# Keys and values of two chunks in one load: a retention layer with a SoLU network behind it

## The chip, the cores and the metric

The kernel runs on one core of a Trainium2 chip. The metric is the device time of one launch in microseconds (us), as the median of several runs. Beside the timed runs one execution was profiled; its span goes from the first to the last instruction of the program.

## What is computed

For 8 batches and 8 heads, with 576 positions of head size 64, the attention part is a retention layer: scores with a decay per head, causal, no softmax. Its output becomes 4608 tokens of 512 channels, which pass through a network with a SoLU activation and a layer norm:

```
scores = q @ k.T / sqrt(64)
ret    = scores * gamma[h] ** (i - j)      # for i >= j, otherwise 0
x      = ret @ v                           # tokens x 512, heads side by side
h      = x @ w_in                          # 512 -> 1024
solu   = h * softmax(h)
ln     = (solu - mean) / sqrt(var + 1e-6) * g_ln
out    = ln @ w_out                        # 1024 -> 512
```

All inputs and the output are 32-bit floats. Inside, matmul operands are 16-bit floats.

## The kernel before

The work is cut into 36 chunks of 128 tokens. Batches go in four pairs, and each pair has nine chunks: for each of four blocks of 128 positions one chunk of the first batch and one of the second, then a ninth chunk that holds the last 64 positions of both. Chunks 0 to 8 are the first pair, 9 to 17 the second, and so on. Chunks 9 and 10 are thus the same positions of two neighbouring batches, as are 11 and 12, 13 and 14, 15 and 16; chunk 17 stands alone. The decay is carried from block to block by a state of each batch, so a chunk does not need earlier keys and values.

The order of everything is written out by hand in `ORDER`, a list of steps such as `ck:9:g` (step `ck` of chunk 9 on engine g; a is ScalarE, v VectorE, g GpSimd). There is no loop: the list is run from left to right, and each engine takes its instructions in that order. The steps that matter here:

- `ld` loads queries, keys and values of a chunk into three buffers (`qf`, `kf`, `vf`), three DMAs on SyncE's queue, in this order. SyncE also issues the stores of the output (`st`) and the transposes of 16-bit keys by DMA (`kd`, from chunk 12 on).
- `cq`, `ck`, `cv` scale and convert queries, keys and values to 16 bits, mostly on GpSimd (POOL in the profile); they free the loaded buffer.
- `tq`/`tr` turn queries (and keys) on TensorE; `sc` makes the scores, `mk` masks them on VectorE (DVE), `av` multiplies by the values, `fs` adds the product of the queries with the state, and `dk` on POOL makes that state in 16 bits.
- `ex` copies the result out of PSUM, `m1` is the product with `w_in`, `mx`, `xp` and `so` make the maximum, the exponential and the activation, `tu` and `eu` turn it, `sq`, `ra` and `rp` make the norm, `m2` is the product with `w_out`, and `st` scales on ScalarE (ACT) and stores. `rp` is the step that the profile shows as line 583.

The buffers of a name form a ring whose places are also written out: `SLOTS` lists, for each new buffer, which place it takes, and `BANKS` does the same for the four PSUM banks that are not kept for `h`. A step whose place still has a reader waits for it. Loaded buffers of 2 KB per partition: seven for queries, six for keys, seven for values.

The order around the change, with the first loads that it touches (`ld:12`, `ld:9`, `ld:10`, `ld:11`):

```
... ld:7 tu:2 wo:7:g wo:0:a ld:8 wo:5:a
sq:2 ra:1:g tu:4 mk:6 rp:1 ld:12 mx:3 ld:9 eu:2:v m2:1 sq:0 dk:6 ld:10 dk:4 sq:4 cq:8:g eu:4:v
m2:0 cq:7:v st:1 ck:7:a xp:3 ra:0:v cv:7:v mx:5 so:3 mm:0 ld:11 rp:0 st:0 ...
... cv:8:g eq:8:a ... ck:9:g rp:4 sq:3 kv:7 eu:3:a m2:3 cq:9:g ... dk:7 ... cq:11:v ...
```

A key or value load moves rows of 64 floats (256 bytes); a query load (but for chunk 34) moves rows of 1 KB, since four tokens of a head lie together there.

Of the kernel before, what the change touches and what calls it, by code (L numbers as in the profile page):

```python
# [10 lines left out]
FP = mybir.dt.float32  # L11
F16 = mybir.dt.float16
BF16 = mybir.dt.bfloat16
P = 128
H = 8
D = 64
# [3 lines left out]

PLAIN = 5
BY_DMA = 12
BY_PE = (15, 20)
ORDER = """
c1:0 ld:1 ld:0 cq:1:g cv:1:v ck:1:a cq:0:g tq:1 eq:1:av wu:2:2 wu:5:2 ck:0:a cv:0:g sc:1 ld:2 mk:1
# [16 lines left out]
so:7 av:9 sq:6 ex:9:a tr:10 er:10:a cv:10:g ad:9 d3:9 ra:6:v rp:6 cq:13:g sq:7 ra:7:g ck:13:g  # L42
kd:13 m2:6 st:6 mx:8 cv:13:g tu:7 eu:7:a sc:10 mk:10 m1:9 kv:10 ad:10 dk:10 tr:11 xp:8 so:8 av:10
ex:10:a tr:12 er:12:v cv:12:g er:11:a m2:7 tu:8 dk:9 sc:11 mx:9 m1:10 cv:11:g mk:11 av:11 fs:11
ld:15 sq:8 rp:7 ra:8:v eu:8:a kv:11 d3:10 xp:9 cq:17:g rp:8 ex:11:a st:7 m2:8 so:9 tu:9 ad:11
d3:11 dk:11 mx:10 sc:12 cq:14:g ck:14:a kd:14 sq:9 m1:11 eu:9:v xp:10 ck:15:g ld:16 st:8 kv:12
mk:12 ld:19 ra:9:v cv:17:g tr:14 er:14:a tr:13 ad:12 dk:12 so:10 av:12 fs:12 ex:12:a cv:14:g
er:13:a m2:9 sc:13 mx:11 rp:9 xp:11 mk:13 cq:16:g tu:10 eu:10:a ck:17:v m1:12 so:11 sc:14 st:9
mk:14 av:13 ck:16:g sq:10 fs:13 ex:13:a m2:10 ra:10:g rp:10 mx:12 d3:12 kv:13 ad:13 cq:15:g tu:11
# [40 lines left out]
"""  # L90

BANKS = """
01231023102130121321302130213023110231012320132012302301320310312031201320321021312310210231032032
10230123012031203123123031231023102301201023012021032103213013021301023102130213013202130213012103
130132132132130210321032132123230212103201032301231031
"""

RINGS = dict(
    qf=7, kf=6, vf=7, q16=5, k16=6, v16=5, qkT=4, ret0=4, ret1=4, xT=4, t=4, s16=4, s32=4, h=2,
    e=3, u=5, uT=5, o_sb=4,  # L100
)
SLOTS = """
qf 012345601234560135426015324601532460
kf 012345012345012453014523014520314520
vf 012345601234560134625016342051346250
q16 012340123401324103123041203412304132
v16 012341023410234132012041320421320413
k16 012345120345102341502314053210452310
# [40 lines left out]
def kernel(  # L149
# [10 lines left out]
    nc = tc.nc  # L160
# [11 lines left out]
    load = ctx.enter_context(tc.tile_pool(name="load", bufs=6))  # L172
# [10 lines left out]
    chunks = []  # L183
# [6 lines left out]
    def tokens(src, n):  # L190

        bs, c = chunks[n]
        if c < 4:
            return src[bs[0], :, c * P : (c + 1) * P, :].rearrange("h t d -> t h d")
        return src[bs[0] : bs[1] + 1, :, 4 * P :, :].rearrange("b h t d -> t b h d")

    def fours(src, n):

        bs, c = chunks[n]
        if c < 4:  # L200
            return src[bs[0], :, c * P : (c + 1) * P, :].rearrange(
                "(g h) (t a) d -> t g h (a d)", h=2, a=4
            )
        return src[bs[0] : bs[1] + 1, :, 4 * P :, :].rearrange(
            "b (g h) (t a) d -> t b g h (a d)", h=2, a=4
        )
# [25 lines left out]
    def ring(pool, shape, dtype, name):  # L232

        at = int(next(slots[name]))
        assert at < RINGS[name]
        return pool.tile(shape, dtype, tag=f"{name}_{at}", name=name, bufs=1)
# [5 lines left out]
    T = {}  # L242
# [20 lines left out]
    def quads(n):  # L263

        return n != NCH - 2

    def ld(n):

        for key, src in (("qf", q), ("kf", k), ("vf", v)):
            dst = ring(load, [P, H, D], FP, key)  # L270
            if key == "qf" and quads(n) or key == "kf" and chunks[n][1] == 4:
                nc.sync.dma_start(  # L272
                    out=dst.rearrange("p (h a) d -> p h (a d)", h=2), in_=fours(src, n)
                )
            else:
                nc.sync.dma_start(out=dst, in_=tokens(src, n))  # L276
            T[key, n] = dst

    def scaled(n, key, out, table, engine):
# [35 lines left out]
    def tq(n):  # L315

        tp = bank([P, 2, 4, P], F16, "tp")
        for i, src in enumerate((T.pop(("q16", n)), T["k16", n])):
            s2 = src.rearrange("p h d -> p (h d)")
            for hp in range(4):  # L320
                turn(tp[:, i, hp], s2[:, hp * P : (hp + 1) * P])
        T["tp", n] = tp

    def kd(n):
        if chunks[n][1] == 4 or n < BY_DMA or n in BY_PE:
            return
        T["qkT", n] = ring(att, [P, 2, 4, P], F16, "qkT")
        nc.sync.dma_start_transpose(
            out=T["qkT", n][:, 1], in_=T["k16", n].rearrange("p h d -> p (h d)")
        )  # L330
# [6 lines left out]
    def tr(n):  # L337
        if chunks[n][1] == 4 or n < BY_DMA or n in BY_PE:
            return tq(n)
        tp = bank([P, 4, P], F16, "tr")  # L340
        s2 = T.pop(("q16", n)).rearrange("p h d -> p (h d)")
        for hp in range(4):
            turn(tp[:, hp], s2[:, hp * P : (hp + 1) * P])
        T["tp", n] = tp

    def er(n, e="a"):
        if chunks[n][1] == 4 or n < BY_DMA or n in BY_PE:
            return eq(n, e)
        turned(ENG[e], n, T["qkT", n][:, 0], T.pop(("tp", n)))
# [15 lines left out]
    def eq(n, e="v"):  # L365

        qkT = ring(att, [P, 2, 4, P], F16, "qkT")
        tp = T.pop(("tp", n))
        turned(ENG[e[0]], n, qkT[:, 0], tp[:, 0])
        if chunks[n][1] == 4:  # L370
            turned(ENG[e[-1]], n, qkT[:, 1], tp[:, 1])
        else:
            copy(ENG[e[-1]], qkT[:, 1], tp[:, 1])
        T["qkT", n] = qkT
# [493 lines left out]
```

## Time and profile before

| | us |
|---|---|
| median of 3 runs | 212.56 |
| lowest, highest | 212.26, 213.14 |
| the profiled execution | 211.63 |
| its span | 209.9 |
| TensorE's mean granted clock in it | 0.99 |

The profiled execution is 0.93 us faster than the median of the runs. The page gives each engine's busy time, the span in 40 slices of 5.2 us, the DMA queues, and the chain of work that ended last. PE is TensorE, PEld its weight loads, DVE VectorE, ACT ScalarE, POOL GpSimd, SP SyncE. In a timeline a row has its start and length in us, engine, line, operation, output and inputs, and in brackets the idle time before it and what ended that. Names are cut: `q`, `k` and `v` are the 16-bit tensors, `s` the state, `rs` the result of `rp`.

### The profile page before, as it was taken

What the parts mean: (1) busy time and instruction counts of PE and PEld (TensorE: products, weight loads), DVE (VectorE), ACT (ScalarE), POOL (GpSimd) and SP (SyncE); (2) the same over time, 40 slices, a digit from 0 to 9 for tenths busy, and PEclk for the clock granted to TensorE, in tenths of its full rate; (3) what the DMA queues carried; (4) which work ended last, traced back from release to release, by engine and by line L of the source; (5) the groups of instructions that cost most, each with busy time, mean ns of one, the idle gap of its engine ahead of it and who ended that gap; (6) DMA issues with size and microseconds to landing.
All of it is one profiled execution on the core that took longest, in us unless ns stands there. A gap on an engine that the chain in (4) does not pass through costs nothing.

```text
span 209.9 us, 7674 instructions
## 1 busy us (share of the span) xinstructions
PE 196.1 (93%) x3173; PEld 124.8 (59%) x3173; DVE 178.3 (85%) x312; ACT 167.9 (80%) x289; POOL 166.2 (79%) x244
## 2 busy tenths in 40 slices
PE   0887699999999999999999999999999999999993
PEld 0464457665756666667656656676666666565552
DVE  0476979999998899979898899999989998999650
ACT  2424769999779997988899788888798897798982
POOL 5395979978799998896938999799999984938531
PEclk9999889999999999999999999999999999999999
DMA  5999999999999999999999899999999995999264
GB/s 133 262 342 274 257 201 355 241 244 249 227 267 279 218 212 247 265 192 253 181 276 221 159 224 231 223 229 228 174 263 233 173 196 153 194 188 242 67 219 153
DMA packets 107859, 46.94 MB, mean 224 GB/s; under 512 B 91560, under 2 KB 101808, under 8 KB 107824
## 3 DMA queue, kind: packets, MB, share of 16 engines
q1 hardware_dynamic: 107504, 46.28, 98.3%
q8 instruction: 25, 0.41, 0.9%
q10 hardware_dynamic: 320, 0.16, 0.3%
q14 instruction: 10, 0.08, 0.1%
HBM read 32.54 MB, written 9.44 MB: 200 GB/s over the span
## 4 chain that ended last, share of the span: by engine, by line
PE 83%; SPq 5%; DMA 4%; DVE 3%; POOL 2%; issue 0%; ACT 0%; DVEq 0%
PE o L258 29%; PE h L258 27%; PE lp L253 6%; PE sc L383 5%; DMA qf<-in_q_dram 4%; PE x L458 4%; PE x L258 3%; PE tp L253 3%; PE tr L253 2%; SPq L276 2%; PE kp L407 2%; SPq L272 2%; SPq L781 1%; DVE ret L396 1%; DVE nm L514 1%; POOL q L292 1%
## 5 line engine op out<-in xcount | busy, mean ns | idle before, releaser
L258 PE MATMUL h<-w_in,xT 128*64 128x512 f16 x560 | 67.8, 384 | 0.3 <-DVE w_in L245 0.3
L258 PE MATMUL o<-w_c,uT 128*64 128x512 f16 x480 | 56.8, 380 | 0.0
L396 DVE TENSOR_TENSOR ret<-sc,tris 128x512 f16<-128x512 f32 x72 | 46.2, 682 | 4.2 <-PE sc L383 4.2
L258 PEld LDWEIGHTS <-xT 128*64 128x64 f16 x576 | 32.0, 112 | 24.1 <-issue 2.0
L520 ACT ACTIVATE e<-h,nm 128x1024 f32<-128x1024 f32 x35 | 39.3, 1122 | 7.6 <-DVE nm L514 6.5
L514 DVE TENSOR_REDUCE nm<-h 128x1 f32<-128x1024 f32 x35 | 42.6, 1217 | 1.8 <-PE h L258 1.6
L258 PEld LDWEIGHTS <-uT 128*64 128x64 f16 x560 | 30.0, 110 | 23.6
L529 DVE SCALAR_TENSOR_TENSOR u<-h,e 128x1024 f16<-128x1024 f32 x35 | 42.6, 1218 | 1.3 <-ACT e L520 0.8
L292 POOL TENSOR_TENSOR q<-qf,small 128x512 f16<-128x512 f32 x31 | 32.6, 1056 | 6.8 <-DMA qf<-in_q_dram 6.8
L434 POOL TENSOR_TENSOR s<-t,small 128x512 f16<-128x512 f32 x32 | 33.8, 1061 | 3.8 <-DVE t L422 3.6
L557 ACT ACTIVATE sq<-u,su 128x1024 bf16<-128x1024 f16 x30 | 34.6, 1153 | 1.2 <-DVE u L529 1.1
L281 POOL TENSOR_TENSOR v<-vf,small 128x512 f16<-128x512 f32 x32 | 33.8, 1061 | 1.4 <-DMA vf<-in_v_dram 1.3
L617 ACT ACTIVATE o_sb<-o,rs 128x512 f32<-128x512 f32 x35 | 24.1, 693 | 5.9 <-POOL rs L583 3.6
L583 POOL TENSOR_TENSOR rs<-w,mhalf 128x1 f32<-128x1 f32 x36 | 20.8, 580 | 7.1 <-DVE w L574 3.8
L245 ACT CAST xT<-x 128x512 f16<-128x512 f32 x32 | 18.6, 587 | 6.8 <-PE x L258 5.4
L245 ACT COPY uT<-lp 128x1024 f16<-128x1024 f16 x17 | 17.3, 1017 | 0.7 <-PE lp L253 0.7
L253 PE MATMUL lp<-ident,u 128*64 128x128 f16 x448 | 17.0, 220 | 0.1
L245 POOL CAST k<-kf 128x512 f16<-128x512 f32 x24 | 14.6, 610 | 2.8 <-DMA kf<-in_k_dram 2.5
L458 PE MATMUL x<-ret,v 128*64 128x128 f16 x288 | 14.9, 225 | 1.4 <-DVE ret L396 1.3
L253 PEld LDWEIGHTS <-q 128*64 128x64 f16 x280 | 10.9, 116 | 8.8 <-POOL q L292 6.4
L446 POOL TENSOR_TENSOR s<-t,small 128x256 f32<-128x256 f32 x24 | 14.9, 623 | 1.5 <-DVE t L422 1.5
L245 ACT COPY qkT<-tp 128x512 f16<-128x512 f16 x24 | 13.1, 592 | 3.5 <-PE tp L253 3.5
(88 smaller groups left out, 268.1 us busy)
## 6 DMA issues: line engine op xcount, KB each, us to landing
qf<-in_q_dram SPq DMA_DIRECT2D x36, 256.0 KB, 4.4
kf<-in_k_dram SPq DMA_DIRECT2D x36, 256.0 KB, 4.7
vf<-in_v_dram SPq DMA_DIRECT2D x36, 256.0 KB, 5.2
out_dram<-o_sb SPq DMA_DIRECT2D x35, 256.0 KB, 4.5
w_in<-in_moe_w_in_dram SPq DMA_DIRECT2D x4, 512.0 KB, 5.7
w_out<-in_moe_w_out_dram SPq DMA_DIRECT2D x4, 512.0 KB, 6.1
qkT<-k SPq DMA_TRANSPOSE x19, 4.1
out_dram<-o_sbh ACTq DMA_DIRECT2D x2, 64.0 KB, 2.1
```

Source lines behind the costliest of these rows:

```text
L245: (engine.copy if engine is nc.scalar else engine.tensor_copy)(out=out, in_=in_)
L253: nc.tensor.transpose(out=out[w], in_=in_[:, w], identity=ident)
L258: nc.tensor.matmul(out=out[w], lhsT=lhsT[:, w], rhs=rhs, start=start, stop=stop, skip_group_check=True,)
L281: engine.tensor_tensor(out=dst, in0=T.pop((key, n)), in1=table.unsqueeze(2).to_broadcast([P, H, D]), op=ALU.mult,)
L292: ENG[e].tensor_tensor(out=dst.rearrange("p (a h) d -> p h a d", h=2), in0=T.pop(("qf", n)).rearrange("p (h a) d -> p h a d", h=2), in1=ta ...
L396: nc.vector.tensor_tensor(out=r, in0=s, in1=m, op=ALU.mult)
L434: nc.gpsimd.tensor_tensor(out=s16, in0=t.unsqueeze(2).to_broadcast([P, 4, 2, D]), in1=gd.unsqueeze(3).to_broadcast([P, 4, 2, D]), op=ALU.mult,
L514: nc.vector.tensor_reduce(out=nm, in_=T["h", n], axis=AX.X, op=ALU.max, negate=True)
L520: nc.scalar.activation(out=e, in_=T["h", n], func=ACT.Exp, bias=T.pop(("nm", n)), accum_out=s)
L529: nc.vector.scalar_tensor_tensor(out=u, in0=T.pop(("h", n)), scalar=-1.0, in1=T.pop(("e", n)), op0=ALU.mult, op1=ALU.mult, accum_out=su,)
L557: nc.scalar.activation(out=s, in_=T.pop(("v", n)), func=ACT.Square, scale=-float(DFF), bias=T.pop(("su", n)), accum_out=ss,)
L617: nc.scalar.activation(out=o_sb, in_=T.pop(("o", n)), func=ACT.Copy, scale=T.pop(("rs", n)))
```

## The change

From chunk 9 on, the keys of two chunks of one pair of batches (9 and 10, 11 and 12, ...) are loaded by one DMA of 512 KB, and their values by another. The joined loads go out at the `ld` step of whichever chunk of the two comes first in `ORDER`; the other chunk's `ld` issues its queries alone. Ninth chunks, and all chunks below 9, are loaded as before, though into buffers that hold pairs. These are four for keys and four for values, each for two chunks, and queries have six places. One step is moved: `ld:16` stands right behind `ld:15`. `SLOTS` is written anew for the three names and `BANKS` from its 64th entry on. The order of the instructions on TensorE, VectorE, ScalarE and GpSimd is unchanged; SyncE issues 24 DMAs fewer.

```diff
+BY_TWO = 9
...
-ld:15 sq:8 rp:7 ra:8:v eu:8:a kv:11 d3:10 xp:9 cq:17:g rp:8 ex:11:a st:7 m2:8 so:9 tu:9 ad:11
-d3:11 dk:11 mx:10 sc:12 cq:14:g ck:14:a kd:14 sq:9 m1:11 eu:9:v xp:10 ck:15:g ld:16 st:8 kv:12
+ld:15 ld:16 sq:8 rp:7 ra:8:v eu:8:a kv:11 d3:10 xp:9 cq:17:g rp:8 ex:11:a st:7 m2:8 so:9 tu:9
+ad:11 d3:11 dk:11 mx:10 sc:12 cq:14:g ck:14:a kd:14 sq:9 m1:11 eu:9:v xp:10 ck:15:g st:8 kv:12
...
 RINGS = dict(
-    qf=7, kf=6, vf=7, q16=5, k16=6, v16=5, qkT=4, ret0=4, ret1=4, xT=4, t=4, s16=4, s32=4, h=2,
+    qf=6, kf=4, vf=4, q16=5, k16=6, v16=5, qkT=4, ret0=4, ret1=4, xT=4, t=4, s16=4, s32=4, h=2,
...
+    def pair(n):
+
+        return (n,) if chunks[n][1] == 4 else (n - n % 9 % 2, n - n % 9 % 2 + 1)
+
     def ld(n):
 
+        bs, c = chunks[n]
         for key, src in (("qf", q), ("kf", k), ("vf", v)):
-            dst = ring(load, [P, H, D], FP, key)
-            if key == "qf" and quads(n) or key == "kf" and chunks[n][1] == 4:
+            if key == "qf":
+                dst = ring(load, [P, H, D], FP, key)
+            else:
+                if ("two", key, n) not in T:
+                    two = ring(load, [P, 2, H, D], FP, key)
+                    for i, m in enumerate(pair(n)):
+                        T["two", key, m] = two, i
+                both, i = T["two", key, n]
+                dst = both[:, i]
+            if key == "qf" and quads(n) or key == "kf" and c == 4:
                 nc.sync.dma_start(
                     out=dst.rearrange("p (h a) d -> p h (a d)", h=2), in_=fours(src, n)
                 )
-            else:
+            elif key == "qf" or n < BY_TWO or c == 4:
                 nc.sync.dma_start(out=dst, in_=tokens(src, n))
+            elif (key, pair(n)) not in T:
+                T[key, pair(n)] = True
+                b0 = chunks[pair(n)[0]][0][0]
+                nc.sync.dma_start(
+                    out=both.rearrange("p b h d -> p (b h) d"),
+                    in_=src[b0 : b0 + 2, :, c * P : (c + 1) * P, :].rearrange("b h t d -> t (b h) d"),
+                )
             T[key, n] = dst
```

More of the change, by code (lines that the diff above doesn't have):

```diff
@@ L92 @@
 BANKS = """
-01231023102130121321302130213023110231012320132012302301320310312031201320321021312310210231032032
-10230123012031203123123031231023102301201023012021032103213013021301023102130213013202130213012103
-130132132132130210321032132123230212103201032301231031
+01231023102130121321302130213023110231012320132012302301320310321032102310312012321320120132031031
+20130213021032103213213032132013201302102013021012031203123023012302013201230123023101230123021203
+230231231231230120312031231213130121203102031302132032
 """
 RINGS = dict(
-    qf=7, kf=6, vf=7, q16=5, k16=6, v16=5, qkT=4, ret0=4, ret1=4, xT=4, t=4, s16=4, s32=4, h=2,
+    qf=6, kf=4, vf=4, q16=5, k16=6, v16=5, qkT=4, ret0=4, ret1=4, xT=4, t=4, s16=4, s32=4, h=2,
     e=3, u=5, uT=5, o_sb=4,
@@ L102 @@
 SLOTS = """
-qf 012345601234560135426015324601532460
-kf 012345012345012453014523014520314520
-vf 012345601234560134625016342051346250
+qf 012345012345012405312450132450132450
+kf 01230123021302130231
+vf 01230123021032102310
 q16 012340123401324103123041203412304132
```

## The prediction

> **What bounds the kernel now.** I read the page first (busy shares, the row of 40 slices, the chain that ended last), then the table of stages, then the timelines of PE, POOL and DVE around the first joined loads, and last the loads one by one with their time to landing.
>
> ```profile
> span 209.9 us, 7674 instructions
> ...
> PE 196.1 (93%) x3173; PEld 124.8 (59%) x3173; DVE 178.3 (85%) x312; ACT 167.9 (80%) x289; POOL 166.2 (79%) x244
> ...
> PE   0887699999999999999999999999999999999993
> ...
> PE 83%; SPq 5%; DMA 4%; DVE 3%; POOL 2%; issue 0%; ACT 0%; DVEq 0%
> ```
>
> The slices show PE short of work only in the first six (31 us) and in the last one. The chain agrees: 83% PE, and SP and DMA together 9%, which is the wait for the first loads. The table of stages says the same in us (columns: length, then busy time of PE, PEld, DVE, ACT, POOL, then clock, DMA share, GB/s):
>
> ```profile
> 40.00:60.00 20.00, 20.00 (x328) 12.79 (x326) 19.69 (x38) 17.80 (x32) 16.39 (x24) 1.00 0.97 234
> 60.00:80.00 20.00, 20.00 (x344) 12.77 (x340) 18.12 (x34) 17.65 (x31) 19.83 (x28) 1.00 1.08 244
> ```
>
> From 40 us on PE is busy all the time at full clock. So no load can make the middle shorter by coming earlier; it can only make it longer by coming too late. POOL (19.83 of 20) and DVE (19.69 of 20) are nearly full too, so what they lose there they do not soon win back. The DMA engines are full as well (0.97, 1.08): a transfer put ahead of another delays it by its own length.
>
> **What the change does to the queue.** Loads of chunks 0 to 8 keep order and size, so the first 41 us stay. Engines other than SP keep their instructions and order. The first load call that changes is chunk 12's, whose joined loads bring keys and values of 11 and 12; chunk 9's bring 9 and 10. SP now issues: queries 12, keys 11+12, values 11+12, queries 9, keys 9+10, values 9+10, queries 10, the store of chunk 1, queries 11. Before, it was 12 (three loads), 9 (three), 10 (three), the store, 11 (three). Counted in transfers of 256 KB, ahead of the moment when keys 9 may be used there are now three more (keys 11, values 11, and keys 10 in the same load); ahead of queries 11 there are two more (keys and values 11; 10's were there already).
>
> What a transfer costs in the full queue comes from the loads' own rows (start of issue in us; below it the time from there to landing), for values 8, keys 9, queries 11 and values 11:
>
> ```profile
> L276 SPq DMA_DIRECT2D vf<-in_v_dram x1: 643/643/643, 41.0 to 41.0; - x1
> ...
> DMA to landing us min/median/max: 5.1/5.1/5.1
> ...
> L276 SPq DMA_DIRECT2D kf<-in_k_dram x1: 558/558/558, 46.8 to 46.8; - x1
> ...
> DMA to landing us min/median/max: 4.2/4.2/4.2
> ...
> L272 SPq DMA_DIRECT2D qf<-in_q_dram x1: 607/607/607, 53.8 to 53.8; - x1
> ...
> DMA to landing us min/median/max: 3.4/3.4/3.4
> ...
> L276 SPq DMA_DIRECT2D vf<-in_v_dram x1: 581/581/581, 55.1 to 55.1; - x1
> ...
> DMA to landing us min/median/max: 5.9/5.9/5.9
> ```
>
> They land at 46.1, 51.0, 57.2 and 61.0. From values 8 to keys 9 five transfers of 256 KB land in 4.9 us (queries, keys, values 12, queries and keys 9), to queries 11 eleven in 11.1: 1.0 us each. But the two after queries 11 (keys and values 11) take 3.8: the queue loses 1.8 us somewhere between 57.2 and 61.0. So:
>
> - Keys 9 land at 51.0 + 3 x 1.0 = 54.0 (53.4 if each costs 0.8; 55.8 if a pause of 1.8 falls among them).
> - Queries 11 land at 57.2 + 2 x 1.0 = 59.2, inside the stretch where the queue lost 1.8 us. If that loss stays at its place in time they land at 61.0, if it falls behind them at 59.2. The loss is known only to lie within those 3.8 us, so I take a value near the middle: 60.0.
>
> The Trainium skill speaks for the change here: "DMA: Bandwidth & Descriptors", Anatomy of one DMA, gives a fixed cost of about 2.0 us for each DMA beside bytes / 436e3, fitted for GpSimd's path, and its Rules for kernel authors advise joining small transfers. Charged one after the other this would be an estimated 2.6 us for 256 KB and 3.2 us for 512 KB, so a joined load would save 2.0 us and four of them would undo the delay. The trace disagrees: 1.0 us from landing to landing leaves no room for 2.0 us each, so in a full queue that time overlaps. The sum goes on from 1.0 us.
>
> **What waits for keys 9.** POOL's timeline (start, length, line, output; idle time before it in brackets): values 8, keys 9, the power for chunk 4, queries 9, the state of chunk 7.
>
> ```profile
> 49.63 1.22 POOL L281 TENSOR_TENSOR v<-vf,small 128x512 f16<-128x512 f32 x1
> 50.99 0.61 POOL L245 CAST k<-kf 128x512 f16<-128x512 f32 x1
> 52.69 0.66 POOL L583 TENSOR_TENSOR rs<-w,mhalf 128x1 f32<-128x1 f32 x1 [1.08 <-DVE w L572]
> 53.32 1.04 POOL L292 TENSOR_TENSOR q<-qf,small 128x512 f16<-128x512 f32 x1
> 55.22 1.04 POOL L434 TENSOR_TENSOR s<-t,small 128x512 f16<-128x512 f32 x1 [0.86 <-DVE t L422]
> ```
>
> The cast starts the moment the keys land: no slack. With keys at 54.0 it ends at 54.6; the power follows there (52.69 before), queries 9 at 55.2, the state at 56.3 instead of 55.22, ending at 57.3 instead of 56.3. The idle 1.08 and 0.86 swallow 1.94 of the 3.0 us; about 1.0 us of lag remains on POOL. ACT's store of chunk 4 needs the power:
>
> ```profile
> 54.54 0.70 ACT L617 ACTIVATE o_sb<-o,rs 128x512 f32<-128x512 f32 x1
> 56.58 0.59 ACT L245 CAST xT<-x 128x512 f16<-128x512 f32 x1 [1.33 <-PE x L258]
> ```
>
> It moves to about 55.3 and still ends before 56.58: cover of 1.33 us. If the keys take until 55.8 that cover is gone and ACT starts 0.4 us or so late. PE:
>
> ```profile
> 57.04 0.61 PE L258 MATMUL x<-qkT,s 128*64 128x64 f16 x16
> ...
> 64.13 0.39 PE L458 MATMUL x<-ret,v 128*64 128x128 f16 x8
> ```
>
> The first row is chunk 8's product with the state that POOL now ends at 57.3: PE stands still for 0.3 us (nothing at 53.4, 2.0 us at 55.8).
>
> **What waits for queries 11.** They are scaled on DVE, whose rows are queries 11, the two maskings of chunk 9, and the next idle moment:
>
> ```profile
> 57.89 0.68 DVE L292 TENSOR_TENSOR q<-qf,small 128x512 f16<-128x512 f32 x1
> ...
> 62.65 1.28 DVE L396 TENSOR_TENSOR ret<-sc,tris 128x512 f16<-128x512 f32 x2
> ...
> 67.51 1.29 DVE L396 TENSOR_TENSOR ret<-sc,tris 128x512 f16<-128x512 f32 x2 [0.53 <-PE sc L383]
> ```
>
> Slack to the load: 57.9 - 57.2 = 0.7 us. With queries at 60.0 DVE stands for 2.1 us (1.3 at 59.2, 3.1 at 61.0), and queued behind are the centring of the second weight, chunk 8's cast, chunk 6's product, chunk 7's maximum and the maskings, with no idle time up to 67.5. The maskings end at 63.9 and PE takes their result at 64.13: 0.2 us of slack. So PE is late there by 2.1 - 0.2 = 1.9 us (1.1 to 2.9). The two waits do not add up: PE's 0.3 us at 57 is contained in the later 1.9, since DVE is late by the load's own time, not by PE's.
>
> **What comes after.** Every later pair delays its first chunk's keys by 1.0 us, its values and all up to the second chunk's queries by 2.0 us. Loads are mostly converted later than that after landing, and from 64 us on all engines run 1.9 us later while the loads mostly do not, which covers the shortest slacks. I cost those pairs at nothing; without the cover, keys 15, which land just before their cast, would cost POOL 1.0 us. SP issues 24 DMAs fewer, 24 x 0.6 = 14 us of its time (the rows above have 0.56 to 0.64 each): worth nothing while PE is full. The smaller rings hold nothing up: keys 9 and 10, for one, take the pair of buffers of chunks 4 and 5, which were converted long before. The new PSUM banks change which instruction PE waits for in two places, and both of these have ended well before. As PE has no idle time afterwards, the 1.9 us stay to the end.
>
> **Sum.** The profiled execution took 211.63 us (span 209.9 and 1.7 around it); with 0.3 and another 1.6 it is 213.5. The median of the runs is 212.56, 0.9 above the profiled one, so I forecast 212.56 + 1.9 = 214.5 us.
>
> **Rivals.**
>
> 1. *Loads late, PE not* (no change). If two joined halves ride for less, or DVE's lag is swallowed, nothing happens. It decides at queries 11: landed by 58.1 there is no lag (0.45 us for each added transfer), by 59.1 the loss is within what can be told. For it: 59.2 without the pause is close to that edge. Against: 256 B rows stay 256 B rows, and 0.45 us is half of any mean above. 212.6 to 213.6; chance 0.25.
>
> 2. *The queue runs dry.* A joined load lists twice as many rows; if its list only goes out when the one before has drained, the engines idle at each. At 1.0 us for each of the four joined loads ahead of queries 11, DVE would be late by 6.1 us: 212.56 + 5.9 = 218.5. Against it, nothing in the trace shows a gap behind a long list. Chance 0.08.
>
> 3. *Faster.* SP is free 14 us earlier in sum, so key transposes and stores go out sooner. For it: DMA engines and SP are busy together. Against: PE waited for none of that after 40 us; the few tenths it ever lost are the most that can return: 212.3 at best, or under 211.5 only if the head changed. Chance of over 0.5%: 0.04.
>
> 4. *PE catches up.* "Perfetto Trace Analysis" of the Trainium skill, Identifying the Most-Contended Engine, holds matmul busy time for a bad measure of how close PE is to its limit. If PE had such room, it would regain the 1.9 us by closing ranks, and the time would be 212.6, as in rival 1. In the chain the 16 matmuls of one product take 1.73 us, and no other product in it takes less:
>
> ```profile
> 58.10 1.73 PE h L258 x16
> ```
>
> So I see no room, and give it no chance beyond rival 1's.
>
> **How the numbers follow.** The forecast has 0.63: its bounds on PE's lag, 1.1 to 2.9, give 213.7 to 215.5, and to 216.6 if a second pause hits keys 9 and ACT too. A measurement of this kernel tells about 0.5% (1.06 us) from no change. Slower by more: 0.63 + 0.08 = 0.71; within: 0.25; faster: 0.04. The range from 212.6 to 216.6 leaves out the dry queue and the best part of rivals 1 and 3.
>
> **What would show it.** In the profile after: POOL idle before the keys cast near 51, ended by the load, about 3 us; DVE idle before queries 11 near 58, ended by the load, 1.3 to 3 us; PE idle near 57 and 64, and none later; SP's queue without gaps; landings of joined loads 2.0 us apart. I am wrong if PE shows no idle time at 55 to 68, if the loss sits at later pairs, or if joined loads land less than 1.5 us after the transfer before.

## The result, and the profile after

| | before | after |
|---|---|---|
| median, us (lowest, highest; 4 runs each) | 212.85 (212.26, 213.47) | 216.25 (215.27, 216.81) |
| after / before | | 1.0149, 95% interval 1.0110 to 1.0189 |
| the profiled execution, us | 211.63 | 216.81 |
| its span, us | 209.9 | 215.1 |

The change costs 3.4 us by the medians (2.3 to 4.0 by the interval); 214.5 was forecast, with 212.6 to 216.6 as the range. The two profiled executions lie further apart, 5.18 us: after's is the slowest of its four, before's lies 1.2 us below its median. Sizes read from the two traces are therefore those of this pair, and the experiments give the others. Ratios leave out executions that the records show as disturbed, which matters for one kernel below.

The page after: span, busy shares, PE in 40 slices, and the chain that ended last.

```profile
span 215.1 us, 7641 instructions
...
PE 196.9 (92%) x3173; PEld 124.8 (58%) x3173; DVE 180.3 (84%) x312; ACT 168.7 (78%) x289; POOL 165.7 (77%) x244
...
PE   0897699799799999999999999999999999999993
...
PE 62%; DMA 15%; SPq 8%; DVE 6%; POOL 4%; ACT 2%; issue 1%; DVEq 0%; POOLq 0%; ACTq 0%
```

PE's work is the same (3173 matmuls, 196.9 us beside 196.1), the span is 5.2 us longer, and the chain is no longer PE's alone: DMA went from 4% to 15%. The slices show two sevens after the head, in the slices from 37.6 and from 53.8 us. The first is a wait for `w_out`, ahead of all that is changed; it used up what had been won in the head. The second is new. The table of stages (length, then busy time of PE, PEld, DVE, ACT, POOL, then clock, DMA share, GB/s) places it and finds a second one:

```profile
55.00:70.00 15.00, 13.05 (x218) 8.34 (x216) 11.96 (x24) 9.69 (x18) 13.65 (x19) 1.00 0.98 242
70.00:150.00 80.00, 79.90 (x1422) 51.79 (x1418) 73.97 (x127) 70.54 (x120) 70.37 (x95) 1.00 1.07 214
150.00:170.00 20.00, 19.58 (x290) 12.07 (x288) 17.54 (x28) 16.72 (x28) 18.43 (x31) 1.00 1.00 221
170.00:190.00 20.00, 19.59 (x318) 11.91 (x316) 19.27 (x30) 16.05 (x29) 14.49 (x21) 1.00 0.90 168
```

```profile
55.00:70.00 15.00, 15.00 (x278) 10.04 (x274) 13.57 (x26) 12.12 (x21) 14.35 (x20) 1.00 0.98 257
70.00:150.00 80.00, 79.90 (x1400) 51.53 (x1396) 74.48 (x128) 70.54 (x119) 70.42 (x96) 1.00 1.09 220
150.00:170.00 20.00, 20.00 (x350) 13.34 (x348) 18.88 (x31) 17.25 (x31) 19.22 (x30) 1.00 1.05 229
170.00:190.00 20.00, 20.00 (x294) 11.67 (x292) 19.21 (x30) 16.91 (x32) 12.01 (x21) 1.00 0.96 182
```

The first four rows are after's, the second four before's. In the 80 us in between nothing is lost (79.90 in both). Since matmul ends are modelled, these sums undercount; better is to compare the start of one and the same matmul in both traces, which works because PE's order is the same. At 54 us after is 0.5 us late, from the head (before's `o<-w_out` of 52.31 starts at 52.82). The loss of the early stage, in the timelines of POOL, ACT, PE and DVE after:

```profile
55.99 0.61 POOL L246 CAST k<-kf 128x512 f16<-128x512 f32 x1 [4.62 <-DMA kf<-in_k_dram]
56.56 0.55 POOL L604 TENSOR_TENSOR rs<-w,mhalf 128x1 f32<-128x1 f32 x1
57.08 1.04 POOL L313 TENSOR_TENSOR q<-qf,small 128x512 f16<-128x512 f32 x1
58.08 1.29 POOL L455 TENSOR_TENSOR s<-t,small 128x512 f16<-128x512 f32 x1
```

```profile
57.15 0.69 ACT L638 ACTIVATE o_sb<-o,rs 128x512 f32<-128x512 f32 x1 [1.98 <-POOL rs L604]
```

```profile
57.88 0.41 PE L479 MATMUL x<-ret,v 128*64 128x128 f16 x8 [0.40 <-ACT o_sb L638]
59.43 0.58 PE L259 MATMUL x<-qkT,s 128*64 128x64 f16 x14 [1.07 <-POOL s L455]
64.12 0.64 PE L254 MATMUL lp<-ident,u 128*64 128x128 f16 x16 [0.21 <-DVE u L550]
67.38 0.38 PE L479 MATMUL x<-ret,v 128*64 128x128 f16 x7 [0.27 <-DVE ret L417]
```

```profile
61.30 0.69 DVE L313 TENSOR_TENSOR q<-qf,small 128x512 f16<-128x512 f32 x1 [2.83 <-DMA qf<-in_q_dram]
```

All waits of the prediction are there, in its order: POOL stands for the keys of 9, ACT then stands for the power that POOL makes behind them, PE for ACT's read and for the state, DVE for queries 11, and PE again behind DVE. The product with the state (its third matmul, ahead of which PE stood) was at 57.07 before and is at 59.43 now, the product with the values at 64.13 before and at 67.38 now: late by 2.4 and by 3.25. Less the head's 0.42 (what a product with `w_out` that starts at 41.02 us before is late by) the early stage costs 2.8 us.

The second loss is at the end. Two waits of DVE for loads, of values 29 and queries 31:

```profile
154.49 1.38 DVE L302 TENSOR_TENSOR v<-vf,small 128x512 f16<-128x512 f32 x1 [0.98 <-DMA vf<-in_v_dram]
168.48 0.82 DVE L313 TENSOR_TENSOR q<-qf,small 128x512 f16<-128x512 f32 x1 [1.37 <-DMA qf<-in_q_dram]
```

One product with `w_out` ahead of them starts at 150.83 before and 154.07 after; a key product behind them, `kp`, at 168.70 and 173.91: late by 3.24 and by 5.21, so 2.0 us are lost here. 0.4 + 2.8 + 2.0 is the whole difference.

### The profile page after: what moved, and what is told of

Read it like the earlier page. It is cut to its first block, busy times and chain, and to the rows that moved or that the text cites. A ratio compares the mean times of both kernels' runs of the same rounds, so it can differ in the third digit from the quotient of the medians.

```text
span 215.1 us, 7641 instructions
## 1 busy us (share of the span) xinstructions
PE 196.9 (92%) x3173; PEld 124.8 (58%) x3173; DVE 180.3 (84%) x312; ACT 168.7 (78%) x289; POOL 165.7 (77%) x244
## 4 chain that ended last, share of the span: by engine, by line
PE 62%; DMA 15%; SPq 8%; DVE 6%; POOL 4%; ACT 2%; issue 1%; DVEq 0%; POOLq 0%; ACTq 0%
PE o L259 23%; PE h L259 20%; DMA qf<-in_q_dram 8%; PE lp L254 4%; DMA w_out<-in_moe_w_out_dram 4%; PE sc L404 4%; DMA kf<-in_k_dram 3%; PE x L479 3%; SPq L290 2%; PE x L259 2%; SPq L286 2%; SPq L812 2%; PE tr L254 2%; SPq L802 1%; PE tp L254 1%; PE kp L428 1%
## 5 line engine op out<-in xcount | busy, mean ns | idle before, releaser
L259 PE MATMUL h<-w_in,xT 128*64 128x512 f16 x560 | 66.6, 380 | 0.8 <-DVE w_in L246 0.8
L259 PEld LDWEIGHTS <-xT 128*64 128x64 f16 x576 | 31.3, 110 | 23.9 <-issue 1.1
L259 PEld LDWEIGHTS <-uT 128*64 128x64 f16 x560 | 30.5, 110 | 25.0 <-DVE ret L417 1.5
L313 POOL TENSOR_TENSOR q<-qf,small 128x512 f16<-128x512 f32 x31 | 32.1, 1042 | 6.3 <-DMA qf<-in_q_dram 6.3
L254 PEld LDWEIGHTS <-u 128*64 128x64 f16 x448 | 14.3, 110 | 3.1 <-DVE u L550 1.1
```

The lines of the kernel that those rows point to most:

```text
L254: nc.tensor.transpose(out=out[w], in_=in_[:, w], identity=ident)
L259: nc.tensor.matmul(out=out[w], lhsT=lhsT[:, w], rhs=rhs, start=start, stop=stop, skip_group_check=True,)
L313: ENG[e].tensor_tensor(out=dst.rearrange("p (a h) d -> p h a d", h=2), in0=T.pop(("qf", n)).rearrange("p (h a) d -> p h a d", h=2), in1=ta ...
```

## The experiments

My theory: joined loads put bytes ahead of transfers that were just in time; two places lose for it, each by itself, and nothing else of the change (rings, banks, the moved load step, fewer DMAs) matters. The rivals are in the expectations. Where a time is given as late, it is the start of the same matmul against before's trace.

### No joins, all else changed

```diff
-BY_TWO = 9
+BY_TWO = 36
```

> The changed kernel with every load of 256 KB again, each into its half of a pair buffer; the rings, the places, the PSUM banks and the moved load of chunk 16 stay changed. Theory (the joined loads make keys 9, queries 11 and a few later loads late): back to the kernel before, 212.3 to 213.3 us, no wait of POOL for keys near 51 us, none of DVE for queries near 58. Rival (buffers, banks or the moved load cost the time): stays near 216.2 us.

213.41 us (ratio 1.0021, 0.9968 to 1.0074). After the head PE waits nowhere:

```profile
55.00:70.00 15.00, 15.00 (x260) 9.83 (x256) 14.26 (x27) 12.26 (x22) 13.70 (x20) 1.00 1.07 267
...
150.00:170.00 20.00, 20.00 (x349) 13.12 (x345) 18.73 (x31) 17.26 (x31) 18.64 (x31) 1.00 1.09 217
```

Buffers of pairs, six places for queries, the new banks and the moved step cost nothing that shows. The loss is the joins'.

### Joined from 18 on, and joined from 9 to 17 alone

```diff
-BY_TWO = 9
+BY_TWO = 18
```

> Joined loads only from chunk 18 on. Theory: the 2.8 us that PE lost between 56 and 68 us are gone and only the waits for values 29 and queries 31 are left, about 1.0 us each in the profile: 213.3 to 214.8 us. Rival (long loads cost everywhere a little): two thirds of the whole loss, about 214.9 us, spread over the span.

214.56 us (1.0082, 1.0023 to 1.0140). PE has its waits at 152 to 168 us, late by 1.1 and another 0.9 us, and none at 56 to 68.

```diff
-            elif key == "qf" or n < BY_TWO or c == 4:
+            elif key == "qf" or n < BY_TWO or n >= 18 or c == 4:
```

> Joined loads only for chunks 9 to 16, single ones from 18 on. Theory: PE loses about 2.8 us between 56 and 68 us and nothing later: 215.0 to 216.0 us. Rival (long loads cost everywhere a little): one third of the loss, about 213.8 us.

214.00 us (1.0045, 1.0004 to 1.0085), less than I expected, since the early loss was smaller here. PE, then DVE:

```profile
58.18 0.58 PE L259 MATMUL x<-qkT,s 128*64 128x64 f16 x14 [0.33 <-POOL s L455]
62.84 0.64 PE L254 MATMUL lp<-ident,u 128*64 128x128 f16 x16 [0.18 <-DVE u L550]
66.09 0.38 PE L479 MATMUL x<-ret,v 128*64 128x128 f16 x7 [0.26 <-DVE ret L417]
```

```profile
59.98 0.72 DVE L313 TENSOR_TENSOR q<-qf,small 128x512 f16<-128x512 f32 x1 [1.51 <-DMA qf<-in_q_dram]
```

The same loads in the same order, but queries 11 land 1.3 us earlier than in the changed kernel, and PE's product at 64.13 before is late by 1.96, 1.45 of it not from the head (0.51). The two parts are thus separable: early joins give the early loss, later joins the late one. By its time alone this kernel is where the rival (a little everywhere) put it, at 213.8, and the one above not far from the rival's 214.9; what speaks against that rival is the place: from 70 to 150 us PE's lag stays the same to 0.02 us in both. The early loss has no fixed size.

### The same bytes in the same order, as two loads of 256 KB

The chunk that is needed first goes first.

```diff
-                nc.sync.dma_start(
-                    out=both.rearrange("p b h d -> p (b h) d"),
-                    in_=src[b0 : b0 + 2, :, c * P : (c + 1) * P, :].rearrange("b h t d -> t (b h) d"),
-                )
+                first = both[:, i], both[:, 1 - i]
+                for part, m in zip(first, (n, sum(pair(n)) - n)):
+                    nc.sync.dma_start(out=part, in_=tokens(src, m))
```

> The queue order of the changed kernel, but each joined load as two loads of 256 KB one behind the other, the chunk that is needed first in front. Theory (bytes put ahead count, not the length of a load): queries 11 land as late as in the changed kernel, near 61 us, DVE waits as long; keys 9 land about 1.1 us sooner, so POOL's wait shrinks from 4.6 to about 3.5 us; 215.3 to 216.3 us. Rival (a load of 512 KB is slow in itself): near 213 us, with transfers landing closer together.

216.92 us (1.0193, 1.0147 to 1.0239), as slow as the changed kernel. So the loss does not need a long load, nor that its first half is released only with its second; what the order puts ahead of what is enough. The parts are not the same, though. Keys 9 landed at 52.98 (55.94 in the changed kernel), POOL waited 1.78 us, less than I expected, and PE did not stand for the state behind them; queries 11 landed at 60.21, and PE lost 2.2 us in this stage, most of it behind DVE. At the end it lost 2.8. The waits in 140 to 180 us that loads end:

```profile
DVE q L312 <- DMA qf<-in_q_dram: 1.5, 1, 1.5
POOL q L312 <- DMA qf<-in_q_dram: 1.5, 1, 1.5
```

### Needed loads first: 9, 10, 11, 12

```diff
-sq:2 ra:1:g tu:4 mk:6 rp:1 ld:12 mx:3 ld:9 eu:2:v m2:1 sq:0 dk:6 ld:10 dk:4 sq:4 cq:8:g eu:4:v
-m2:0 cq:7:v st:1 ck:7:a xp:3 ra:0:v cv:7:v mx:5 so:3 mm:0 ld:11 rp:0 st:0 tq:7 mc:0:v av:6 ld:13
+sq:2 ra:1:g tu:4 mk:6 rp:1 ld:9 mx:3 ld:10 eu:2:v m2:1 sq:0 dk:6 ld:11 dk:4 sq:4 cq:8:g eu:4:v
+m2:0 cq:7:v st:1 ck:7:a xp:3 ra:0:v cv:7:v mx:5 so:3 mm:0 ld:12 rp:0 st:0 tq:7 mc:0:v av:6 ld:13
```

(and the places in `SLOTS` to suit).

> The changed kernel with the load steps of the second group in the order 9, 10, 11, 12 in place of 12, 9, 10, 11 (places of the rings exchanged to match). Keys 9 and 10 go out right behind values 8, queries 11 ahead of the joined load of 11 and 12. Theory: keys 9 land near 49 us and queries 11 near 54, both before their use; the loss between 56 and 68 us is gone, the late one (values 29, queries 31) stays or moves: 213.0 to 214.8 us. Rival (long loads cost in themselves): stays over 215.5 us.

214.87 us (1.0133, 1.0047 to 1.0220; the profiled execution took 213.86).

```profile
55.00:70.00 15.00, 15.00 (x271) 9.89 (x269) 13.57 (x26) 12.26 (x21) 14.05 (x20) 1.00 1.13 271
...
150.00:170.00 20.00, 19.19 (x300) 11.91 (x296) 17.18 (x28) 16.51 (x30) 18.53 (x31) 1.00 1.00 223
```

The early loss is gone with all loads still joined, and the late one is there (2.0 us by starts). The late loss thus does not come from the early lag.

### The late joins apart: with that order, and with the order of the change

```diff
-            elif key == "qf" or n < BY_TWO or c == 4:
+            elif key == "qf" or n < BY_TWO or n >= 27 or c == 4:
```

With the order of the experiment above:

> As the run with the order 9, 10, 11, 12, and loads from chunk 27 on are single again; chunks 9 to 25 stay joined. Theory: neither loss is left and joining eight pairs costs nothing, but brings nothing either, since PE has no idle time to give back: 212.2 to 213.2 us, the same as the kernel before. Rival (fewer issues on SP are worth something): under 212.0 us.

212.43 us (1.0004, 0.9972 to 1.0036; 10 runs): neither loss, with chunks 9 to 25 joined. In the profile 1.7 us were lost once, at 85 us, behind a late key transpose:

```profile
PE sc L404 <- DMA qkT<-k: 1.6, 1, 1.6
```

Whether other executions have this wait is not shown; in this one PE had come out of the head 1.3 us ahead of before. Even without the two losses the kernel is not faster than before. With the order of the change:

> Chunks 9 to 26 joined as in the change, chunks from 27 on loaded singly (order of the changed kernel). My theory (two separate losses: about 2.8 us of PE's time at 56 to 68 us from keys 9 and queries 11, about 2.0 us at 152 to 168 us from values 29 and queries 31): the second goes, the first stays; 214.0 to 215.2 us beside a kernel before of 212.7, PE's waits at 57 to 64 us as in the changed kernel and none ended by a load after 150 us. Rival (the late loss is a consequence of the lag from the early one, or of the pool of pairs, and not of the joined loads there): it stays, 216 us or more. Rival (the middle joins, 18 to 26, cost too): a loss between 68 and 150 us of 0.5 us or more.

214.82 us (1.0104, 1.0065 to 1.0143).

```profile
55.00:70.00 15.00, 13.99 (x246) 9.26 (x243) 13.41 (x24) 11.16 (x20) 13.95 (x19) 1.00 1.00 249
...
150.00:170.00 20.00, 20.00 (x322) 12.70 (x320) 18.72 (x30) 17.32 (x31) 16.22 (x27) 1.00 1.14 228
```

The early loss stays (1.4 us by starts), the late one is gone but for 0.4 at 170 us. The two are independent.

### One of the two early waits at a time

Queries 11 ahead of chunk 12's loads, keys 9 as late as in the change:

```diff
-sq:2 ra:1:g tu:4 mk:6 rp:1 ld:12 mx:3 ld:9 eu:2:v m2:1 sq:0 dk:6 ld:10 dk:4 sq:4 cq:8:g eu:4:v
+sq:2 ra:1:g tu:4 mk:6 rp:1 ld:11 ld:12 mx:3 ld:9 eu:2:v m2:1 sq:0 dk:6 ld:10 dk:4 sq:4 cq:8:g eu:4:v
```

> The changed kernel with the load step of chunk 11 right ahead of chunk 12's: queries 11 go out first, all else as before, so keys 9 come one transfer later still. Theory: DVE no longer waits for queries 11; POOL waits for keys 9 about 5.5 us, and PE's loss comes from POOL alone, through the power of chunk 4 and the state of chunk 7: about 2.3 us between 56 and 60 us, nothing at 64 to 68; 214.8 to 216.3 us. If DVE's wait alone set the loss: 213.5 us.

216.95 us (1.0228, 1.0158 to 1.0299). DVE does not wait for queries 11, POOL waits 4.26 us for keys 9, and PE loses 1.85 us up to one product, 1.5 of them there:

```profile
59.08 0.58 PE L259 MATMUL x<-qkT,s 128*64 128x64 f16 x14 [1.34 <-POOL s L455]
```

Keys 9 ahead, queries 11 as late as in the change:

```diff
-sq:2 ra:1:g tu:4 mk:6 rp:1 ld:12 mx:3 ld:9 eu:2:v m2:1 sq:0 dk:6 ld:10 dk:4 sq:4 cq:8:g eu:4:v
+sq:2 ra:1:g tu:4 mk:6 rp:1 ld:9 mx:3 ld:12 eu:2:v m2:1 sq:0 dk:6 ld:10 dk:4 sq:4 cq:8:g eu:4:v
```

> The changed kernel with the load step of chunk 9 ahead of chunk 12's: keys 9 land near 49 us, queries 11 as late as in the changed kernel, near 61. Theory (the two waits do not add, PE's loss there is the larger of the two): POOL does not wait for keys 9, DVE still stands about 3 us before queries 11, and PE loses about 2.8 us, now between 60 and 68 us: 215.0 to 216.5 us. If POOL's wait alone set the loss: about 213.5 us.

> The same kernel as the one with only keys 9 ahead (order 9, 12, 10, 11), for a second profile, because PE's loss of 4 to 5 us at 60 us in the first one is larger than the wait for queries 11 explains. My theory: POOL does not wait for keys 9; DVE waits 1.5 to 3.5 us for queries 11; PE loses 1.5 to 3 us between 58 and 68 us through DVE alone, and about 2.0 us at 152 to 168 us; 215.2 to 216.4 us. Rival (queries 11 cost nothing by themselves, the early loss is POOL's): PE loses under 0.5 us at 56 to 68 us, 214.3 to 215.0 us.

Run twice: 215.88 us (1.0154, 1.0083 to 1.0225; profiled execution 218.69) and, from two executions, a ratio of 1.0218 (1.0160 to 1.0276; profiled execution 217.72). POOL does not wait. DVE, then PE, then the clock, of the second:

```profile
62.62 0.69 DVE L313 TENSOR_TENSOR q<-qf,small 128x512 f16<-128x512 f32 x1 [4.16 <-DMA qf<-in_q_dram]
```

```profile
64.54 1.63 PE L259 MATMUL o<-w_c,uT 128*64 128x512 f16 x10 [3.61 <-DVE w_c L844]
```

```profile
65.00:67.00 2.00, 1.89 (x22) 0.97 (x20) 2.00 (x5) 0.69 (x1) 1.52 (x2) 0.58 1.24 269
67.00:69.00 2.00, 2.00 (x24) 1.04 (x21) 2.00 (x4) 1.27 (x3) 0.00 (x0) 0.57 1.02 351
69.00:71.00 2.00, 2.00 (x46) 1.40 (x44) 2.00 (x5) 1.50 (x3) 0.00 (x0) 1.00 1.13 250
```

My numbers for it were too low: queries 11 came later than in any other kernel, and through DVE alone PE lost 3.9 us, to which the clock added 1.7 (late by 0.4 at 41 us, by 4.2 at the product above, by 6.0 at 69 us). The late loss, which I expected too, was not there in this profile: with the engines 6.0 us late the last loads came in time. The profile of the first run has an even longer standstill, and part of the late loss:

```profile
64.74 1.87 PE L259 MATMUL o<-w_c,uT 128*64 128x512 f16 x7 [4.11 <-DVE w_c L844]
```

```profile
156.87 1.59 DVE L302 TENSOR_TENSOR v<-vf,small 128x512 f16<-128x512 f32 x1 [0.77 <-DMA vf<-in_v_dram]
```

There the engines were 5.8 us late, DVE waited for values 29 all the same, and PE lost 1.2 us behind it. Either early wait alone is enough to make PE late, so taking one away is worth nothing; taking both away, above, is worth all of the early loss.

## Why the prediction was right, and where it was not

**What bounds it** (PE from 40 us; only losses possible): held. The kernel with neither of the two losses came out level with before (1.0004).

**Transfers of 1.0 us.** Too low. Without a pause 512 KB took 2.3 us from landing to landing (queries 12, keys 11 + 12 and values 11 + 12 at 46.77, 49.06 and 51.34 us), so 1.14 for each half, and a pause fell among those ahead of keys 9. (The pause in the trace before could have been placed more closely than the prediction does: keys 11, with 3.8 us to landing from 54.46, landed near 58.2, so the pause lies behind them.) The share of the DMA engines and what they moved, 40 to 66 us in 40 slices of 0.65, after and then before:

```profile
DMA  4498699999999999999999981469658999999999
GB/s 81 80 312 230 188 225 279 243 240 283 239 200 209 256 227 176 312 276 257 232 221 225 221 131 31 61 196 402 194 46 251 392 374 297 286 264 202 224 228 234
```

```profile
DMA  1776999999998999999996949996999999999787
GB/s 33 172 242 147 298 268 190 295 283 214 255 160 261 276 269 231 227 279 280 256 227 131 349 80 303 294 228 137 314 335 230 266 288 256 225 381 324 228 238 183
```

After moves 131, 31 and 61 GB/s in the three slices from 54.95, and 46 from 58.85, at which the loads land late; before's lowest between 41 and 66 us is 80. So keys 9 came at 55.94, beyond the upper bound of 55.8, and ACT's cover of 1.33 us went, as the text said it would there (ACT waited 1.98, PE 0.40 for ACT). Queries 11 came at 61.27, against 60.0 (61.0 at most).

**PE late by DVE's lag less 0.2, and the waits not adding up.** Held, with more than one dose. DVE's row of queries 11 is late against before's 57.89, less the head, by 61.30 - 57.89 - 0.42 = 2.99 us in the changed kernel, 59.98 - 57.89 - 0.51 = 1.58 with 9 to 17 alone; less 0.2 that gives 2.8 and 1.4, and PE lost 2.8 and 1.45. POOL's wait, 1.85 us for PE in the kernel where it stands alone, is contained in it.

**Later pairs at nothing.** This step failed, and it is the larger part of what was missed. The text's own sign against itself, a loss at later pairs, came true for 2.0 us: 2.0 to 2.2 in the profiles of the changed kernel, of joins from 18 on, of the needed order and of queries 11 ahead, 2.8 with two loads for one, 1.2 and nothing in the two profiles of keys 9 ahead (engines 5.8 and 6.0 us late), and at most 0.4 where chunks from 27 on are loaded singly. I had counted bytes and taken the lag as cover, and had given SP's shorter list as worth nothing. What I left out is when SP can issue. SP's rows after (start of issue, length) of values 29 + 30, the store behind them, queries 30, values 31 + 32 and two stores:

```profile
144.51 3.90 SPq L294 DMA_DIRECT2D vf<-in_v_dram  x1
148.51 3.64 SPq L644 DMA_DIRECT2D out_dram<-o_sb  x1
...
153.54 0.63 SPq L286 DMA_DIRECT2D qf<-in_q_dram  x1
...
156.85 3.31 SPq L294 DMA_DIRECT2D vf<-in_v_dram  x1
160.27 2.42 SPq L644 DMA_DIRECT2D out_dram<-o_sb  x2
```

The issue of a joined load, and of the next DMA, is held for up to 3.9 us. Before, the loads of values 29, 30 and 32 took 0.57 to 0.58 each to issue there (other issues are held in that trace too, the store at 51.02 for 2.69). So queries 31, behind all of these, went out at 164.08 us against 156.85 and landed at 168.45 against 160.31, 8.1 us later. Their slack of 2.4 us (DVE took them at 162.75 before) and DVE's lag of 4.4 make up for 6.8; the rest is the wait of 1.37.

The cover is the part of the step that the runs refute. PE's lag at 150 us was 0.27 us with the needed order, 0.67 with joins from 18 on, 2.30 with queries 11 ahead and 3.24 in the changed kernel, and queries 31 landed at 165.59, 165.89, 167.86 and 168.45: 4.9 to 5.3 us later than before beyond the lag, and the loss was 2.0 to 2.2 in all four. The loads came later along with the engines, so a lag of up to 3.2 us covered nothing. At 5.8 and 6.0 us of lag they landed 3.3 and 2.3 us later beyond it, which DVE did not wait for.

"SP's queue without gaps" was the wrong sign to look for: it has no gaps, but its issues are long. That the hold is by what stands in the queue, and not by a list's length, is suggested by the two-by-two kernel, where SP spent 2.72 us on the two loads of keys 29 and 30 and 2.70 on those of values, against 0.60 and 3.90 for the joined ones. Its queries 31 landed at 167.71 with a lag of 2.47, again 4.9 us later beyond the lag, so the order alone is enough for that lateness. What sets the hold, and how much of the 4.9 us is the hold and how much the bytes ahead, was not tried.

**Sum.** Forecast 1.9; measured 3.4 by the medians. The terms by the traces: early 1.4 (9 to 17 alone, and late joins apart) to 2.8 (the changed kernel's slowest run), late 2.0. The early term was right in place and in size within its bounds; the late one was missing. That the range held is in part luck: the forecast's bounds on PE's lag reach only to 215.5, the median lies above that, and the 1.1 us added for a second pause at keys 9, which no row gives, took in a loss that is not of that pause. The pause did come, but with it the early loss stayed within the bounds.

**Rivals.** *Loads late, PE not*: no, queries 11 landed 2 us beyond the edge given. *The queue runs dry* at each long list: no, the two that went out at 42.87 and 43.52 landed 2.28 us apart, and the holes above are fewer than the joined loads. Whether long lists make holes deeper stays open: from 41 to 66 us the two-by-two kernel has no slice under 114 GB/s, but joins from 18 on, with single loads there too, have one of 72. *Faster*: no. *PE catches up*: no, 3.24 us late at 67 us and 3.24 at 154, so PE regained nothing in 86 us.

## What to carry to other kernels

In a full DMA queue a load costs what lies ahead of it, so before two loads are joined, list what now comes ahead of every transfer that lands just before its use; joining saves issues, and those may be worth nothing. If loads are to be joined, put what is needed first at the head: with the needed order and single loads in the last quarter this kernel was back at its old time, though not below it. Do not count on a lag of the engines as cover: here the loads came later by as much, up to 3.2 us. So follow the issues of the queue too, to the end of the kernel and not only at the first joined load.

## What the runs showed of the hardware

- The load queue has stretches of 1 to 2 us at under 100 GB/s (above), and where they fall differs from kernel to kernel: the same early joins cost 1.4 or 2.8 us. Most come up to 4 us behind a 16 KB packet of the queue that the page lists as instructions (after has 25 of them in 215 us, one at 52.4 us ahead of the hole at 55.0). But about half of all moments of that trace lie as close behind one, and whether it is the cause was not tried.

```profile
q8 instruction: 25, 0.41, 0.8%
```

- A standstill of PE of 3.61 us was followed by 4 us at a granted clock of 0.58 and 0.57 (the rows above) and cost another 1.7 us; the one of 4.11 us, in the other profile of that kernel, has a clock of 0.53 and 0.61 from 64 to 68 us. Standstills of up to 1.59 us from 41 us on in the other kernels had no such sequel (clock 1.00). The Trainium skill, "TensorE: Matmul & The Clock Gate", Part 1, gives about 3.4 us of idling for the fall to half rate and as much for the way back, and the trace agrees. So a late load can cost more than its wait; from which length on, between 1.59 and 3.61 us, no run here shows.
